# Zero fills of two stages as contiguous megabytes, read from DRAM instead of from SBUF

## The chip, the cores and the metric

The kernel runs on one core of one Trainium2 chip. The metric is device time in microseconds (us) for one execution; lower is better. Three executions of the kernel before took 596.52 to 596.76 us, with a median of 596.55 us. The core has five compute engines (TensorE, called PE in the profile; VectorE, DVE; ScalarE, ACT; GpSimd, POOL; SyncE, SP), an on-chip memory (SBUF) of 128 partitions, and 16 DMA engines which carry all data between SBUF and DRAM. A DMA instruction is issued from one of the compute engines' instruction streams and is then carried out by the DMA engines on their own.

## The reference

One decode step of a transformer block and its gradients: layer norms with a modulation computed from `c`, sliding-window attention over the key and value caches, a gated FFN, and then the vector-Jacobian product for ten inputs.

```python
W = min(4096, max(256, Sk // 4))                # Sk = 65536, so W = 4096
k = jnp.repeat(k_cache[:, :, Sk - W:, :], rep, axis=1)
v = jnp.repeat(v_cache[:, :, Sk - W:, :], rep, axis=1)
p = _softmax(jnp.einsum('bhqd,bhkd->bhqk', q, k) * Dh ** (-0.5), axis=-1)
o = jnp.einsum('bhqk,bhkd->bhqd', p, v)
...
_out, _vjp = jax.vjp(_f, A_x, A_k_cache, A_v_cache, A_wq, A_wo, B_w_gate, B_w_up, B_w_down, c, w_mod)
return (out, *_vjp(grad_out))
```

Only the last 4096 of the 65536 rows of each cache take part. The gradients of the two caches, `out_2` and `out_3`, each of shape (1, 4, 65536, 128) in bf16, are therefore zero in the first 61440 rows of each of the four groups: eight regions of 15.7 MB, 126 MB of zeros in all. The kernel has to write them, and half of what it moves is this.

## The kernel before

**Zeros in pieces.** `zeros` is an SBUF tile of 128 partitions by 2048 fp8 zeros (2 KB per partition). Each of the eight regions is seen as 128 rows of 61440 bf16 elements (120 KB); `region[:, i * ZW:(i + 1) * ZW]` with `ZW = 4096` cuts it into 15 pieces. So a piece is 1 MB that consists of 128 rows of 8 KB, with a step of 120 KB from row to row. There are 120 pieces, in the list `zleft`. A fill (L169) writes a piece seen as fp32 from the fp8 tile: the DMA converts each fp8 zero to an fp32 zero, so that 256 KB are read from SBUF and 1 MB is written to DRAM. Seven of the pieces are narrow (`NARROW`): rows 8 to 127 only (L165), preceded by a small DMA (L162), and the rows left out are written by `zero_rest` (L358 and after).

**When a fill is issued.** `zero(n, after)` issues the next n fills of `zleft` from POOL, in order. The first of them waits for the instruction `after`, so that fills are paced by the work of other engines. Lists by stage (`Z_Q`, `Z_SM`, `Z_N`, `Z_B`, `Z_FOLD`, `Z_FFN`, `Z_END`) say how many fills go where. The order of all instructions is written out by hand.

**The stages.** (1) Loads of the caches' windows, `A_wq` and `w_mod`, with transposes and the projection of q; 4 fills. (2) Scores and softmax; 4 fills. (3) The N stage (L640, `n_ps`), four groups by 32 steps: VectorE scales the values by the probabilities (L193), TensorE multiplies them with the keys. `Z_N` spreads 31 fills over its 128 steps; a fill waits for a matmul a few steps back (`recent(mm, 6)`). Loads of `A_wo` stand between (`load_wo`, L338). (4) The B stage (L695, `b_ps`): `bch` multiplies with `A_wo`, 64 chunks of 8 matmuls. `Z_B` spreads 42 fills over it, each behind a matmul (`recent(mm, 3)`), and between them stand loads of sections of `w_mod` (`wm_sec`, L341) and, near the end, of the first FFN tiles (`load_ug`, L869; `load_wd`, L855, issued from SP). Four more fills lie between the chunks, in calls of their own (`Z_GA`, `Z_CB`). (5) The FFN over seven blocks: each loads its tiles, computes, and stores gradients into the same places (`store_ug`, L873; `store_wd`, L858). (6) The end: gradients of the caches' windows, of `wq`, `wo` and `w_mod`, most of them stores of 512 KB and 1 MB, the last ones issued from SP.

POOL issues DMAs in program order, and one that has to wait holds up all behind it. In the trace POOL's DMAs also wait for the landing of an earlier one, the eighth before, so that up to eight are in flight.

Of the kernel before, what the change touches and what calls it, by code (L numbers as in the profile page):

```python
# [10 lines left out]
P = 128  # L11
FP32 = mybir.dt.float32
BF16 = mybir.dt.bfloat16
FP8 = mybir.dt.float8e4
# [23 lines left out]
NARROW = (15, 45, 75, 93, 103, 113, 119)  # L38

def spread(total, n):
    return [(i + 1) * total // n - i * total // n for i in range(n)]
# [10 lines left out]
Z_N = spread(31, 128)  # L53
Z_B = [n + (i in (31, 38)) for i, n in enumerate(spread(29, 43))] + [1, 1, 1, 1, 0] + [1, 0, 0, 1, 1, 1, 0, 0] + [1, 0, 1, 0, 1, 0, 0, 0]
# [4 lines left out]
def kernel(  # L59
# [26 lines left out]
    nc = tc.nc  # L86
    SKW = A_k_cache.shape[2] - W
# [22 lines left out]
    ZW = 4096  # L110
# [9 lines left out]
    ones_f = vt([P, P], "ones_f")  # L120
    nc.vector.memset(ones_f, 1.0)

    zregions = []
    for og in (out_2, out_3):
        for g in range(G):
            region = og[0, g, 0:SKW, :].rearrange("r d -> (r d)").rearrange("(p x) -> p x", p=P)
            for i in range(region.shape[1] // ZW):
                zregions.append(region[:, i * ZW:(i + 1) * ZW])

    narrow = zregions[0:len(NARROW)]
    wide = zregions[len(NARROW):]
    zleft = []
    while narrow or wide:
        if narrow and (len(zleft) in NARROW or not wide):
# [11 lines left out]
    def dep(later, earlier):  # L147
        tc.add_manual_dep(later.ins, earlier.ins.name,
                          mybir.DependencyInfo(mybir.DependencyClass.Sync, mybir.DependencyReason.DATA),
                          reason="pace")  # L150

    def zero(n, after=None):
        for _ in range(n):
            if len(zleft) <= keep[0]:
                return
            region, narrow_ = zleft.pop(0)
            first = None
            if narrow_:
                nc.gpsimd.inc_swdge_sem([], [], mode="reset_dge_cursor")  # L160
                n = nlen - ncount.pop()
                first = nc.gpsimd.dma_start(  # L162
                    out=rest[0:NS, 0:nlen * 128].rearrange("p (t x) -> p t x", t=2)[:, :, n * 64:(n + 1) * 64],
                    in_=zeros[0:NS, 0:64].rearrange("p (t x) -> p t x", t=1).broadcast_to([NS, 2, 64]))
                ins = nc.gpsimd.dma_start(  # L165
                    out=region[8:P, :].bitcast(FP32).rearrange("(t p) x -> p t x", t=2),
                    in_=zeros[0:60, :].rearrange("p (t x) -> p t x", t=1).broadcast_to([60, 2, ZW // 2]))
            else:
                ins = nc.gpsimd.dma_start(out=region.bitcast(FP32), in_=zeros[:, :])  # L169
            if after is not None:  # L170
                dep(first or ins, after)
# [20 lines left out]
    def tt(out, a, b, op):  # L192
        return nc.vector.tensor_tensor(out=out, in0=a, in1=b, op=op)  # L193
# [215 lines left out]
    for j in range(KD):  # L409
        for k in range(16):  # L410
            mm = nc.tensor.matmul(mod_ps[:, k:k + 1], lhsT=wm01_t[j][:, k * P:(k + 1) * P],
                                  rhs=cs_bf[:, j:j + 1], start=(j == 0 and k == 0), stop=(j == KD - 1),
                                  skip_group_check=True)
# [30 lines left out]
    def bank_pair(name, odd):  # L444
        pair = ((ppq, "pq"), (prq, "rq")) if odd % 2 else ((pna, "na"), (pna, "na"))
        return [pl.tile([P, 512], FP32, name=name, tag=tag) for pl, tag in pair]
# [20 lines left out]
    for j in range(KD):  # L467
# [6 lines left out]
        for h in range(HQ):  # L474
            mm = nc.tensor.matmul(q_ps[:, h:h + 1], lhsT=wq_t[j][:, h * P:(h + 1) * P],
                                  rhs=h1_bf[:, j:j + 1], start=(j == 0 and h == 0), stop=(j == KD - 1),
                                  skip_group_check=True)
# [9 lines left out]
    for ch in range(8):  # L487
        ps = new_ps("sc_ps")
        for g in range(G):
            mm = nc.tensor.matmul(ps[32 * g:32 * g + 32, 0:512], lhsT=q_col2[:, HG * g:HG * g + 32],  # L490
                                  rhs=k_T[:, g, ch * 512:(ch + 1) * 512], start=True, stop=True,
                                  tile_position=(0, 32 * g))
# [75 lines left out]
    def ok_cols(ps):  # L568
        cp(ok_f, ps[:, :])
        okv = ok_ps.rearrange("p (a h) -> p a h", a=2)  # L570
        for g in range(G):
            nc.tensor.matmul(okv[:, :, HG * g:HG * g + HG], lhsT=ok_f[:, g * P:(g + 1) * P],
                             rhs=pair_sel[:, :, HG * g:HG * g + HG], start=True, stop=True)

    def ok_rows():
        cp(o_col, ok_ps[:, 0:HQ])
        cp(kb_col, ok_ps[:, HQ:2 * HQ])
        cp(o_bf, o_col)
        lo = scr[:, 768:832].bitcast(FP32)
        for k, (col, rows, s) in enumerate(((o_col, o_rows, 1.0), (kb_col, nkb_rows, -1.0))):  # L580
            st = st_cols[k].rearrange("p (a h) -> p a h", a=4)
            cp(st[:, 0, :], col)
            tt(lo, col, st[:, 0, :], ALU.subtract)
            cp(st[:, 3, :], lo)
            cp(st[:, 1, :], st[:, 3 - 3 * k, :])
            cp(st[:, 2, :], st[:, 3 * k, :])
            rp = new_tp("rp_ok")[:, 0:P]
            nc.tensor.transpose(rp, st_cols[k], ident_bf[:, :])
            nc.scalar.activation(out=rows, in_=rp, func=ACT.Copy, scale=s)

    def build_bd(g):
        for i in range(HG):
            nc.scalar.activation(out=bd[:, i, :], in_=o_rows, func=ACT.Copy,
                                 scale=sel[:, HG * g + i:HG * g + i + 1])
# [30 lines left out]
    def recent(mm, lag):  # L625
        last_mm.append(mm)
        return last_mm[-lag] if len(last_mm) >= lag else last_mm[0]

    for g in range(G):
        nbank = bank_pair("n_ps", g)  # L630
        for t_ in range(KT):
            s = g * KT + t_
            vp = vp_t[(s // 2) % 2]
            if t_ % 2 == 0:
                tt(vp.rearrange("p t h d -> p (t h d)"),
                   v_nat[:, g, t_ * DH:(t_ + 2) * DH].rearrange("p (t o d) -> p t o d", t=2, o=1).broadcast_to([P, 2, HG, DH]),
                   pT2[:, g, HG * t_:HG * t_ + 2 * HG, :].rearrange("p n (o k) -> p n o k", o=1).broadcast_to([P, 2 * HG, 64, 2]),
                   ALU.mult)
            for k in range(2):
                mm = nc.tensor.matmul(nbank[k][:, :], lhsT=k_nat[:, g, t_ * DH:(t_ + 1) * DH],  # L640
                                      rhs=vp[:, t_ % 2, 4 * k:4 * k + 4, :].rearrange("p h d -> p (h d)"),
                                      start=(t_ == 0), stop=False)
            zero(Z_N[s], recent(mm, 6))
            if t_ == 20:
                build_bd(g)
            if s == 2:
                ok_cols(ok4)
            elif s == 4:
                ok_rows()
            elif s == 24:  # L650
                mod_gb((6, 7))
                load_wo(0)
            elif t_ % 2 == 1:
                side()
        for k in range(2):
            nc.tensor.matmul(nbank[k][:, :], lhsT=nkb_rows[:, :], rhs=bd[:, 4 * k:4 * k + 4, :].rearrange("p h d -> p (h d)"),
                             start=False, stop=True)
            c0 = (HG * g + 4 * k) * P
            nc.scalar.activation(out=N_sb[:, c0:c0 + 512], in_=nbank[k][:, :], func=ACT.Copy, scale=float(SCALE))
        load_wo(4 + g)  # L660
        if g < 3:
            jobs.extend(t_unit(h, "AA") for h in range(HG * g, HG * g + HG))
# [5 lines left out]
    bq = []  # L668
# [13 lines left out]
    nbq = len(bq)  # L682
    bbank = {}

    def bch(n=1):
        for _ in range(n):
            if not bq:
                return
            p, i, u = bq.pop(0)
            if i == 0:  # L690
                bbank[p] = bank_pair("b_ps", p)
            for a in range(4):
                h = 4 * u + a
                for k in range(2):
                    mm = nc.tensor.matmul(bbank[p][k][:, :], lhsT=a4[:, p, h, :], rhs=wo_t[u][:, a, k * 512:(k + 1) * 512],  # L695
                                          start=(i == 0 and a == 0), stop=(i == 7 and a == 3))
            zero(Z_B[nbq - 1 - len(bq)], recent(mm, 3))
            if i == 7:
                for k in range(2):
                    o = B_t[p][:, k * 512:(k + 1) * 512]  # L700
                    if k == 0 or p == NBP - 1:
                        nc.scalar.copy(out=o, in_=bbank[p][k][:, :])
                    else:
                        cp(o, bbank[p][k][:, :])
# [649 lines left out]
```

## Time and profile before

| | |
|---|---|
| median of 3 runs | 596.55 us (596.52 to 596.76) |
| span of the profiled execution, first to last instruction | 594.7 us |
| time outside that span, median less span | 1.85 us |
| bytes moved by DMA | 246.61 MB, mean 415 GB/s |
| read from DRAM / written to it | 60.30 MB / 185.60 MB |
| fills of 1 MB (L169) / of 960 KB (L165) | 113 / 7 |
| busy share PE, DVE, ACT, POOL | 68%, 60%, 44%, 27% |

The profile is of one execution. Its page gives busy shares of each engine over the span, a strip of 40 slices of the span for each engine and for the DMA engines, the queues of the DMA engines (q0 is the one POOL issues to, q1 that of SP and ACT), and the chain of work that ended last. A view of DMA traffic can be taken for any stretch of time; its line "DMA packets" counts the packets that ran in it (one packet is one contiguous piece that one DMA engine moves, and small ones of 4 bytes report completion), the MB, and the mean rate. In a line of the timeline or of a group, the text in square brackets or behind the bar is the idle time before the instruction and what ended it; "x3" is a count. "To landing" is the time from the issue of a DMA to the moment that its completion was reported.

### The profile page before, as it was taken

To read this page: it belongs to the slowest core of one execution; us is meant where nothing else is said; L and a number is where in the kernel's file an instruction comes from. 1 tells how busy PE (TensorE), PEld (TensorE's weight loads), DVE (VectorE), ACT (ScalarE), POOL (GpSimd) and SP (SyncE) were. 2 spreads that over 40 slices of the span, in tenths; PEclk is the share of its full clock that TensorE was granted. 3 is DMA by queue.
4 is the path that set the end of the run, shared out by engine and by line. 5 is a ranking of instruction groups with operands and counts; after the bars stand their busy time and mean duration, and the time that the engine had idled before them with its cause. 6 is when DMAs were issued, how large, how long until landed. Compare 5 with 4: busy or idle time off the path is not lost.

```text
span 594.7 us, 10884 instructions
## 1 busy us (share of the span) xinstructions
PE 403.4 (68%) x4492; PEld 270.3 (45%) x4516; DVE 356.9 (60%) x674; ACT 263.3 (44%) x401; POOL 158.8 (27%) x255
## 2 busy tenths in 40 slices
PE   3997688999999989998866236344455283794510
PEld 3995334334344546544446225334344263593410
DVE  3754499999511010086628686686877884868650
ACT  3489514557211014213125375563665832893310
POOL 3113123222222122223221334223344252223200
PEclk9999699999999999999985566555555576855555
DMA  8999999999999999999999999999999999999997
GB/s 350 420 417 422 412 426 415 429 423 426 426 421 426 422 428 425 423 420 426 418 411 414 418 411 416 409 412 408 399 389 417 420 420 424 421 424 423 425 422 330
DMA packets 44049, 246.61 MB, mean 415 GB/s; under 512 B 5141, under 2 KB 5141, under 8 KB 22552
## 3 DMA queue, kind: packets, MB, share of 16 engines
q0 software_dynamic: 36704, 218.64, 95.5%
q1 hardware_dynamic: 7248, 27.27, 13.0%
q8 instruction: 35, 0.57, 0.4%
q14 instruction: 14, 0.11, 0.0%
q10 hardware_dynamic: 48, 0.01, 0.0%
HBM read 60.30 MB, written 185.60 MB: 413 GB/s over the span
## 4 chain that ended last, share of the span: by engine, by line
PE 36%; DMA 30%; DVE 17%; issue 7%; ACT 5%; POOL 0%; ACTq 0%; DVEq 0%; POOLq 0%; SPq 0%
PE b_ps L695 12%; DMA out_dram<-arena 11%; DMA out_dram<-zeros 6%; PE n_ps L640 6%; DMA arena<-in_B_w_gate_dram 6%; DVE arena L210 5%; DVE arena L206 4%; DVE arena L193 4%; DMA arena<-in_B_w_down_dram 3%; DMA arena<-in_w_mod_dram 3%; PE t_ps L602 2%; PE tp_wq L457 2%; PE w_ps L398 1%; PE tp_side L840 1%; PE tp_k L438 1%
## 5 line engine op out<-in xcount | busy, mean ns | idle before, releaser
L695 PE MATMUL b_ps<-arena 128*128 128x512 bf16 x495 | 113.8, 379 | 2.1 <-ACT arena L841 1.1
L169 POOL DMA_DIRECT2D out_dram<-zeros x113 | 61.7, 547 | 174.5 <-DMA out_dram<-zeros 47.7
L841 ACT COPY arena<-tp_side 128x1024 bf16<-128x1024 bf16 x62 | 60.9, 1014 | 71.7 <-PE tp_side L840 71.7
L193 DVE TENSOR_TENSOR arena<-arena 128x2048 bf16<-128x2048 bf16 x64 | 76.6, 1223 | 2.3 <-PE n_ps L640 0.3
L695 PEld LDWEIGHTS <-arena 128*128 128x128 bf16 x512 | 48.7, 98 | 57.6 <-issue 2.9
L210 DVE CUSTOM_DVE_ANT_0 arena<-arena,scr 128x1024 bf16<-128x1024 bf16 x56 | 66.2, 1221 | 9.9 <-ACT scr L1003 9.9
L640 PE MATMUL n_ps<-arena 128*128 128x512 bf16 x249 | 65.0, 378 | 6.9 <-DVE arena L193 5.0
L840 PE MATMUL tp_side<-ident_bf,arena 128*128 128x128 bf16 x496 | 55.2, 289 | 10.3 <-ACT arena L841 5.1
L840 PEld LDWEIGHTS <-arena 128*128 128x128 bf16 x496 | 47.0, 135 | 16.0 <-issue 9.2
L964 PE MATMUL fg<-h_bf,arena 128*128 128x1 bf16 x448 | 15.6, 166 | 43.3 <-DMA arena<-in_B_w_up_dram 25.2
L640 PEld LDWEIGHTS <-arena 128*128 128x128 bf16 x256 | 24.6, 97 | 41.6 <-issue 16.2
L210 DVE CUSTOM_DVE_ANT_0 arena<-arena,b1k 128x1024 bf16<-128x1024 bf16 x24 | 28.4, 1221 | 20.0 <-PE fg L982 19.9
L873 POOL DMA_DIRECT2D out_dram<-arena x28 | 22.1, 796 | 66.5 <-ACT arena L241 47.7
L241 ACT ACTIVATE arena<-scr,h 128x1024 bf16<-128x1024 bf16 x35 | 38.5, 1143 | 2.7 <-DVE dh2acc L210 2.3
L1183 ACT ACTIVATE arena<-ps_kv 128x512 bf16<-128x512 f32 x48 | 26.2, 686 | 22.5 <-PE ps_kv L1179 22.2
L604 ACT CAST arena<-t_ps 128x512 bf16<-128x512 f32 x56 | 30.1, 589 | 12.1 <-PE t_ps L602 12.1
L964 PEld LDWEIGHTS <-arena 128*128 128x128 bf16 x448 | 14.0, 105 | 45.9 <-DMA arena<-in_B_w_up_dram 26.8
L202 DVE CAST arena<-b_ps 128x512 bf16<-128x512 f32 x6 | 4.1, 692 | 51.1 <-PE b_ps L695 51.1
L1179 PE MATMUL ps_kv<-junk,arena 8*128 8x128 bf16 x256 | 27.6, 306 | 7.9 <-DVE arena L206 7.3
L1179 PEld LDWEIGHTS <-arena 8*128 8x128 bf16 x256 | 25.5, 142 | 10.0 <-issue 9.9
L459 ACT COPY arena<-tp_wq 128x1024 bf16<-128x1024 bf16 x23 | 21.7, 1044 | 8.2 <-PE tp_wq L457 8.2
L982 PE MATMUL fg<-hh_bf,arena 128*128 128x1 bf16 x224 | 8.0, 167 | 21.4 <-DMA arena<-in_B_w_down_dram 20.3
(309 smaller groups left out, 637.9 us busy)
## 6 DMA issues: line engine op xcount, KB each, us to landing
out_dram<-zeros POOLq DMA_DIRECT2D x113, 1024.0 KB, 16.4
out_dram<-arena POOLq DMA_DIRECT2D x28, 1024.0 KB, 17.2
out_dram<-arena POOLq DMA_DIRECT2D x30, 512.0 KB, 10.8
out_dram<-arena SPq DMA_DIRECT2D x20, 512.0 KB, 10.0
arena<-in_A_wq_dram POOLq DMA_DIRECT2D x8, 1024.0 KB, 20.4
arena<-in_A_wo_dram POOLq DMA_DIRECT2D x8, 1024.0 KB, 12.9
arena<-in_w_mod_dram POOLq DMA_DIRECT2D x7, 1024.0 KB, 18.6
arena<-in_B_w_up_dram POOLq DMA_DIRECT2D x14, 512.0 KB, 11.4
```

The costliest lines, as they stand in the source:

```text
L169: ins = nc.gpsimd.dma_start(out=region.bitcast(FP32), in_=zeros[:, :])
L193: return nc.vector.tensor_tensor(out=out, in0=a, in1=b, op=op)
L210: return nc.vector.tensor_tensor_reduce(out=out, in0=w, in1=b, scale=1.0, scalar=0.0, op0=ALU.mult, op1=ALU.add, accum_out=acc)
L241: return nc.scalar.activation(out=out, in_=b, func=ACT.Copy, scale=col)
L604: nc.scalar.copy(out=o, in_=ps)
L640: mm = nc.tensor.matmul(nbank[k][:, :], lhsT=k_nat[:, g, t_ * DH:(t_ + 1) * DH], rhs=vp[:, t_ % 2, 4 * k:4 * k + 4, :].rearrange("p h d -> ...
L695: mm = nc.tensor.matmul(bbank[p][k][:, :], lhsT=a4[:, p, h, :], rhs=wo_t[u][:, a, k * 512:(k + 1) * 512], start=(i == 0 and a == 0), stop= ...
L840: nc.tensor.transpose(tp[:, i * P:(i + 1) * P], blk[:, i * P:(i + 1) * P], ident_bf[:, :])
L841: nc.scalar.copy(out=blk if dst is None else dst, in_=tp[:, :])
L964: nc.tensor.matmul(gu[:, col:col + 1], lhsT=ug_v[:, q % 2, j // 4, j % 4, k, f0:f0 + 255:2], rhs=h2_bf[:, j:j + 1], start=(j == 0 and i == ...
L1179: nc.tensor.matmul(ps[:, t4 * DH:(t4 + 1) * DH], lhsT=rows[32 * g:32 * g + HG, t_ * P:(t_ + 1) * P], rhs=hd[32 * g:32 * g + HG, :], start= ...
L1183: nc.scalar.activation(out=o, in_=ps[:, :], func=ACT.Copy, scale=float(scale))
```

## The change

All pieces but those of the first region (`out_2`, group 0) are now contiguous: the region of 15.7 MB is cut into 15 runs of 1 MB (`flat`). The first region keeps its 15 strided pieces, seven of them narrow.

The first contiguous piece, `zero_src`, is the first fill to be issued, as 128 rows of 8 KB from the SBUF tile. `zero` has a new argument, `big`, set in the two calls in the N stage and in `bch`. A contiguous piece that is filled there is not read from the SBUF tile but from the first 256 KB of `zero_src` in DRAM, seen as fp8, and is written as fp32 as before. On both sides the run is contiguous, so that the DMA is made of sixteen pieces that read 16 KB and write 64 KB each, in place of 128 that read 2 KB and write 8 KB. All other contiguous pieces are written as 128 rows of 8 KB from the SBUF tile. The number of fills, where they are issued, what they wait for and the bytes that they write stay as they were.

```diff
-    zregions = []
+    def fill_rows(og, g):
+        return og[0, g, 0:SKW, :].rearrange("r d -> (r d)")
+
+    first_rows = fill_rows(out_2, 0).rearrange("(p x) -> p x", p=P)
+    NZR = first_rows.shape[1] // ZW
+    zregions = [first_rows[:, i * ZW:(i + 1) * ZW] for i in range(NZR)]
+    flat = []
     for og in (out_2, out_3):
         for g in range(G):
-            region = og[0, g, 0:SKW, :].rearrange("r d -> (r d)").rearrange("(p x) -> p x", p=P)
-            for i in range(region.shape[1] // ZW):
-                zregions.append(region[:, i * ZW:(i + 1) * ZW])
+            if og is not out_2 or g:
+                whole = fill_rows(og, g).rearrange("(i x) -> i x", i=NZR)
+                flat.extend(whole[i:i + 1, :] for i in range(NZR))
+
+    zero_src = flat.pop(0)
+    BIGP = 32
+
+    def as_rows(piece, n):
+        return piece.rearrange("i (p x) -> (i p) x", p=n)
+
+    wide = [as_rows(zero_src, P)] + zregions[len(NARROW):] + flat
     narrow = zregions[0:len(NARROW)]
-    wide = zregions[len(NARROW):]
...
-    def zero(n, after=None):
+    def zero(n, after=None, big=False):
...
+            elif big and region.shape[0] == 1:
+                ins = nc.gpsimd.dma_start(
+                    out=as_rows(region, BIGP).bitcast(FP32),
+                    in_=zero_src[:, 0:P * ZW // 4].rearrange("i (p x) -> (i p) x", p=BIGP).bitcast(FP8))
             else:
+                if region.shape[0] == 1:
+                    region = as_rows(region, P)
                 ins = nc.gpsimd.dma_start(out=region.bitcast(FP32), in_=zeros[:, :])
...
-            zero(Z_N[s], recent(mm, 6))
+            zero(Z_N[s], recent(mm, 6), True)
...
-            zero(Z_B[nbq - 1 - len(bq)], recent(mm, 3))
+            zero(Z_B[nbq - 1 - len(bq)], recent(mm, 3), True)
```

## The prediction

> **What bounds the kernel now.** I read the page's strips first, then the waits of the issuing engine, the chain, and last the DMA traffic of single stretches. The strips (40 slices of 14.9 us; the digit is the busy share in tenths) and the totals:
>
> ```profile
> span 594.7 us, 10884 instructions
> PE   3997688999999989998866236344455283794510
> DMA  8999999999999999999999999999999999999997
> GB/s 350 420 417 422 412 426 415 429 423 426 426 421 426 422 428 425 423 420 426 418 411 414 418 411 416 409 412 408 399 389 417 420 420 424 421 424 423 425 422 330
> DMA packets 44049, 246.61 MB, mean 415 GB/s; under 512 B 5141, under 2 KB 5141, under 8 KB 22552
> HBM read 60.30 MB, written 185.60 MB: 413 GB/s over the span
> ```
>
> The reader should see that the DMA engines are busy from end to end at an almost constant rate, while PE is full in only half of the slices. The time is bytes over rate: 246.61 MB at 415 GB/s are the span. Then who holds up the issuing of fills, from 60 to 320 us (us in total, times, longest), and when fills land (first 80 to 120 us, then 160 to 200 us):
>
> ```profile
> POOL out_dram L169 <- DMA out_dram<-zeros: 39.6, 23, 3.9
> POOL out_dram L169 <- PE n_ps L640: 39.3, 18, 5.7
> POOL out_dram L169 <- PE b_ps L695: 24.5, 10, 5.4
> ...
> DMA to landing us min/median/max: 8.8/13.6/15.8
> ...
> DMA to landing us min/median/max: 15.6/17.4/19.5
> ```
>
> Early on PE paces the fills, but a fill still finds at least 8.8 us of work ahead of it, and this backlog grows to 19.5 us, eight DMAs at some 2.45 us each. Then a fill waits for the eighth DMA before it. So the DMA rate, not the issue, sets the progress. The chain shows where this reaches the compute engines:
>
> ```profile
> 251.16 20.51 DMA out_dram<-zeros
> ...
> 271.95 16.91 DMA out_dram<-zeros
> ...
> 289.41 18.56 DMA arena<-in_w_mod_dram
> ...
> 308.02 1.45 PE g_ps L347 x48
> ...
> 542.65 19.39 DMA out_dram<-arena
> ```
>
> Fills that land late hold the `w_mod` load at 289.41 back, and the FFN begins when it has landed. The end is DMA too:
>
> ```profile
> 290.00:300.00 10.00, 7.23 (x55) 3.94 (x54) 9.48 (x14) 3.04 (x3) 2.56 (x5) 1.00 1.15 410
> ...
> 570.00:580.00 10.00, 0.00 (x0) 0.00 (x0) 2.65 (x4) 0.00 (x0) 0.00 (x0) 0.50 1.02 424
> 580.00:590.00 10.00, 0.00 (x0) 0.00 (x0) 0.00 (x0) 0.00 (x0) 0.00 (x0) 0.50 1.01 420
> ```
>
> (From 290 to 300 us, and 570 to 590 us. Columns: stretch, its length, busy time of PE, weight loads, DVE, ACT, POOL, then clock, DMA share, GB/s.) In the last 20 us nothing but DMA runs.
>
> **The change part by part.** *How many fills.* `Z_N` holds 31, `Z_B` 42. In the order of the list one of the 73 is a strided piece of the first region (number 8) and three are narrow (15, 45, 75). 69 fills become large: 69 MB of the 246.6.
>
> *Packets.* This is the term that counts. The traffic of stretches:
>
> ```profile
> DMA packets 1070, 7.70 MB, mean 428 GB/s; under 512 B 119, under 2 KB 119, under 8 KB 142
> ...
> DMA packets 353, 2.60 MB, mean 433 GB/s; under 512 B 36, under 2 KB 36, under 8 KB 36
> ...
> DMA packets 687, 5.01 MB, mean 417 GB/s; under 512 B 78, under 2 KB 78, under 8 KB 78
> ...
> DMA packets 2828, 18.76 MB, mean 426 GB/s; under 512 B 283, under 2 KB 283, under 8 KB 795
> ```
>
> They are 104 to 122 us and 106 to 112 us (fills, almost alone), 24 to 36 us (loads in 8-KB packets), 106 to 150 us (fills and 512 packets of 4 KB). A fill today takes 1,048,576 B / 428 GB/s = 2.450 us. No row shows a 64-KB packet, so its gain is bounded. If a packet costs a fixed time beside its bytes, a large fill saves seven of them on every DMA engine (one packet instead of eight). In 104 to 122 us, 16 engines x 18,000 ns over 928 packets of 8 KB and 23 of half that make 306.5 ns for 8 KB. In 106 to 150 us that price for 2033 packets leaves 704,000 - 623,100 = 80,900 ns for 512 packets: 158 ns for 4 KB. An 8-KB load takes 192,000 / 609 = 315 ns. Twice 158 less 315 is a fixed cost of 1 ns; at 433 GB/s (303 ns for 8 KB) for the fills the same working gives 172 and 29 ns. Seven packets: 7 to 203 ns per fill, 0.5 to 14 us in all; the upper end would be a fill in 2.25 us, 467 GB/s, which no stretch approaches. The row nearest to a fill without interruptions is the best stretch of fills alone, 433 GB/s: 2.422 us, 28 ns less than now. I take that: 69 x 0.028 = **1.9 us** saved.
>
> The Trainium skill bears on this. "DMA: Bandwidth & Descriptors", section "Why small descriptors are slow (HBM only)", states about three cycles of fixed cost per packet, and its section "Where 436 GB/s comes from" a ceiling of 435 GB/s from 16 ports at 850 MHz. By the first, an estimate: 7 x 3 cycles are 25 ns a fill and 1.7 us in all; by the ceiling a fill takes 2.410 us at best and the gain ends at 2.8 us. The trace's 433 GB/s agrees with the ceiling; that 64-KB packets reach it, no row shows.
>
> *Source in DRAM.* 69 x 256 KB = 18.1 MB more are read from DRAM and as much less from SBUF. Price between nothing and, if read bytes counted like written ones, a quarter of a fill, 0.61 us x 69 = 42 us. Stores that read as much as they write (580 to 590 us) run at 420 GB/s, fills that read a quarter at 428: three quarters of the reading cost 2%, and in 24 to 36 us DRAM itself was the source at 417. Reading runs beside writing; I take nothing and keep both ends.
>
> *Dependence.* A large fill needs `zero_src` written. That is the first fill:
>
> ```profile
> 48.88 0.54 POOL L169 DMA_DIRECT2D out_dram<-zeros  x1 [13.45 <-PE q_ps L475]
> ...
> 74.39 0.53 POOL L169 DMA_DIRECT2D out_dram<-zeros  x1 [5.70 <-PE n_ps L640]
> ```
>
> 25 us lie between it and the first fill of the N stage, more than the 19.5 us of the slowest landing above; the wait costs nothing. If its landing were later, the fills and `load_wo` queued behind on POOL would slip, with 8.8 us of backlog to cover it.
>
> *Issue on POOL.* A fill takes 0.53 us of POOL. With fewer packets it should not rise; if it rose to the 0.77 us of a load (the row of 277.15 below), 69 x 0.24 = 17 us of POOL's time would lie under the same backlog. Nothing. *Other contiguous pieces* (35 outside the two calls) keep 8-KB packets with a step of 8 KB instead of 120 KB. Rows with neither step differ from fills by 2% in both directions at most (420 to 433 GB/s); I take nothing. *The calls' order* and the queues' order are unchanged.
>
> *Other queues.* A packet of SP's queue that alternates with POOL's now may stand behind 64 KB, 2.42 us, not 0.31 us. It matters at the handover to the FFN:
>
> ```profile
> 277.15 0.77 POOL L869 DMA_DIRECT2D arena<-in_B_w_up_dram  x1 [1.99 <-DMA out_dram<-zeros]
> 277.90 0.53 POOL L169 DMA_DIRECT2D out_dram<-zeros  x1
> 279.57 0.77 POOL L869 DMA_DIRECT2D arena<-in_B_w_gate_dram  x1 [1.13 <-DMA out_dram<-zeros]
> 281.95 0.53 POOL L169 DMA_DIRECT2D out_dram<-zeros  x1 [1.62 <-PE b_ps L695]
> ...
> 293.30 0.56 POOL L169 DMA_DIRECT2D out_dram<-zeros  x1 [1.16 <-DMA arena<-in_B_w_up_dram]
> ...
> L341 SPq DMA_DIRECT2D arena<-in_w_mod_dram x2: 328/328/328, 287.0 to 293.4; - x2
> ...
> arena<-in_w_mod_dram SPq DMA_DIRECT2D x4, 256.0 KB, 7.8
> ...
> 308.02 1.44 PE L347 MATMUL g_ps<-cs_bf,arena 128*128 128x1 bf16 x48 [2.86 <-DMA arena<-in_w_mod_dram]
> ...
> q8 instruction: 35, 0.57, 0.4%
> PEld L640 <- issue: 16.2, 35, 1.2
> ```
>
> The last SP load is issued at 293.4, lands at about 301.2 and is needed at 308.02. It has 8 packets per DMA engine (256 KB in 2-KB rows). That it lands in 7.8 us where POOL's load at 289.41 needs 18.56 shows that it passes POOL's backlog. At most four of the eight DMAs in flight at 293.4 are fills, so it comes at most 4 x 2.11 = 8.4 us later, at 309.6. It stays hidden or costs 1.6 us; I take nothing. Code is fetched in 35 packets over the span (the row of q8: packets, MB, share); the trace names no wait for one, and PE's unexplained waits in the N stage are 1.2 us at the longest. A fetch 2.4 us late costs nothing under the backlog.
>
> *Sum.* 594.7 - 1.9 = 592.8 us of span. The runs' median stands 1.85 us above the span; 596.55 - 1.9 = **594.6 us**. What is late next: at 308.02 PE had idled 2.86 us, so the FFN can start at most that much earlier before PE is what it waits for. 1.9 us passes; a saving over 2.9 us would in part only shorten the queue, to be gained later in stages that are DMA-bound.
>
> **The rivals.** (1) *No price per packet.* The low end, 1 ns: fills stay at 2.45 us, the change is worth 0 to 0.5 us, 596.3. For it speaks that 8-KB packets already run at 428 to 433; against, that mixtures with 4 KB run slower (426).
>
> (2) *DRAM becomes slower, and the kernel with it.* In fills alone DRAM is written at 428 GB/s and not read; now it would be read at another 107, and sixteen streams stand 64 KB apart in step. The rate of the slowest of the rows above with fills in it, 410 GB/s, makes a fill 2.557 us: 69 x 0.107 = 7.4 us more, 604.0. It decides from 17 ns per fill on (1.2 us, 0.2%). Against it: no row shows that mixing reading with writing costs more than these few per cent. The Trainium skill's "HBM Reference", section "Specifications (TRN2)", speaks for it with an effective 358 GB/s per core and against it with 716 GB/s per domain, which 428 + 107 leaves free; the trace's 428 is already over the first.
>
> (3) *Reading counts in full*: 596.55 + 42.3 = 638.8. Against: the 2% above.
>
> (4) *Late packets of other queues.* If all eight packets of SP's load met a 64-KB one, it would land 8 x 2.11 = 16.9 us later, at 318.1, 10.1 us after it is needed: 606.6. Against: the mixture in flight. The Trainium skill's "DMA: Bandwidth & Descriptors", section "Queues, rings and completion order", has the engines take turns between queues packet by packet; the 7.8 us agree, the price of turns with 64 KB no run here shows.
>
> **How the numbers follow.** A time within 0.2% (1.2 us) can hardly be told from no change on this kernel. Forecast 0.60; (1) 0.13; (2) 0.12; (3) 0.07; (4) 0.08. Faster 0.60, same 0.13, slower 0.27. The forecast's own range is 592 to 595.3: its low end is 4.5 us saved, a fill in 2.385 us. The whole range goes from 591.5 to 601.0 and leaves out (3), half of (2) and (4) and a little below: about 0.2.
>
> **What the profile after would show.** Right: 69 x 112 = 7728 fewer packets on q0; DRAM reading up from 60.3 to about 78.4 MB; 430 GB/s or more in the N and B stages; less waiting of POOL for the eighth DMA before; the `w_mod` load behind the last fills issued about 2 us before 289.41; an end at 420 GB/s as now. Wrong: fills that land later than 19.5 us with a rate below 425 in N and B (2, 3); PE waiting longer than 2.86 us ahead of `g_ps`, for an SP load (4); the same rate as now (1). A wait on each large fill for another large fill's data would overturn everything; the diff has no such overlap.

## The result, and the profile after

The kernel after takes 595.53 us (median of 20 runs, 595.15 to 597.43) against 596.54 us before (20 runs): 1.0 us less, a ratio of 0.9984 with a 95% interval of 0.9978 to 0.9990. It is faster, by a sixth of a per cent, which lies inside the 0.2% that the prediction called hard to tell from no change; only the many runs make it visible. The forecast was 1.9 us less, 594.6 us; 595.53 lies 0.2 us above its own range (592 to 595.3) and inside the whole range (591.5 to 601.0). The profiled execution has a span of 593.8 us, 0.9 us below that of before.

The strips and totals of the page after:

```profile
span 593.8 us, 10908 instructions
PE   3997789999999989998876236344455294894410
DMA  9999999999999999999999999999999999999997
GB/s 351 421 416 422 412 461 393 448 429 427 426 421 403 442 446 411 443 425 402 412 418 402 418 413 414 411 409 405 398 392 418 420 417 426 418 423 426 425 421 328
DMA packets 36321, 246.61 MB, mean 415 GB/s; under 512 B 5141, under 2 KB 5141, under 8 KB 22552
q0 software_dynamic: 28976, 218.64, 91.8%
HBM read 78.39 MB, written 185.60 MB: 445 GB/s over the span
```

The queue of POOL before:

```profile
q0 software_dynamic: 36704, 218.64, 95.5%
```

The bytes that count (246.61 MB) and the small packets are the same. q0 carries 28,976 packets where it carried 36,704: 7728 fewer, 69 x 112. DRAM is read for 18.1 MB more. The strip of GB/s jumps between 393 and 461 in the N and B stages because a packet of 64 KB is counted whole in the slice where it starts; the mean is what can be read. The line "DMA packets" of a stretch counts in the same way: whole packets, those that start in it.

The two long stages, 76 to 300 us: DMA traffic before, then after:

```profile
DMA packets 15209, 94.80 MB, mean 423 GB/s; under 512 B 1661, under 2 KB 1661, under 8 KB 5527
```

```profile
DMA packets 7931, 95.29 MB, mean 425 GB/s; under 512 B 1673, under 2 KB 1673, under 8 KB 5638
```

After has moved 0.49 MB more in the same 224 us. At 425 GB/s this is 1.15 us, some 18 ns for each of the 65 large fills that start in it. Counting a packet that is under way by the share of it that is done, the lead at 300 us is 0.41 MB, 1.0 us, 14 ns for each of the 69. It grows evenly from 0.02 MB at 80 us to 0.24 MB at 180 us and 0.41 MB at 300 us, and it is 0.43 MB at 500 us: the gain is made fill by fill in these stages and then neither lost nor increased.

The chain at the handover to the FFN, and PE's wait there (idle before in brackets), after:

```profile
247.63 19.20 DMA out_dram<-out_dram
267.12 18.36 DMA out_dram<-zeros
...
289.60 17.37 DMA arena<-in_w_mod_dram
307.01 1.45 PE g_ps L364 x48
...
307.01 1.44 PE L364 MATMUL g_ps<-cs_bf,arena 128*128 128x1 bf16 x48 [2.14 <-DMA arena<-in_w_mod_dram]
```

`g_ps` starts at 307.01 instead of 308.02 us: the 1.0 us has arrived. PE still waits 2.14 us for the load, so the limit that the prediction set at 2.86 us was not reached. The `w_mod` load itself is issued no earlier (289.60 against 289.41 us); it lands sooner (17.37 against 18.56 us).

### The profile page after: what moved, and what is told of

Read it like the earlier page. It is cut to its first block, busy times and chain, and to the rows that moved or that the text cites. A ratio compares the mean times of both kernels' runs of the same rounds, so it can differ in the third digit from the quotient of the medians.

```text
span 593.8 us, 10908 instructions
## 1 busy us (share of the span) xinstructions
PE 406.3 (68%) x4516; PEld 271.3 (46%) x4516; DVE 356.7 (60%) x674; ACT 263.6 (44%) x401; POOL 156.2 (26%) x255
## 2 busy tenths in 40 slices
DMA packets 36321, 246.61 MB, mean 415 GB/s; under 512 B 5141, under 2 KB 5141, under 8 KB 22552
## 3 DMA queue, kind: packets, MB, share of 16 engines
q0 software_dynamic: 28976, 218.64, 91.8%
## 4 chain that ended last, share of the span: by engine, by line
DMA 47%; PE 19%; DVE 17%; issue 6%; ACT 5%; POOL 1%; ACTq 0%; DVEq 0%; POOLq 0%; SPq 0%
DMA out_dram<-arena 16%; DMA out_dram<-out_dram 16%; PE n_ps L657 6%; DMA arena<-in_B_w_gate_dram 6%; DVE arena L227 5%; DVE arena L223 5%; DVE arena L210 4%; DMA arena<-in_B_w_down_dram 3%; DMA out_dram<-zeros 3%; DMA arena<-in_w_mod_dram 3%; ACT arena L476 2%; PE t_ps L619 2%; PE w_ps L415 1%; PE tp_k L455 1%; PE b_ps L712 1%
## 5 line engine op out<-in xcount | busy, mean ns | idle before, releaser
L712 PE MATMUL b_ps<-arena 128*128 128x512 bf16 x512 | 115.9, 379 | 1.1 <-ACT arena L858 1.1
L180 POOL DMA_DIRECT2D out_dram<-out_dram x69 | 34.1, 495 | 118.6 <-PE n_ps L657 36.0
L186 POOL DMA_DIRECT2D out_dram<-zeros x44 | 24.8, 565 | 56.8 <-PE q_ps L492 16.1
## 6 DMA issues: line engine op xcount, KB each, us to landing
arena<-in_A_wo_dram POOLq DMA_DIRECT2D x8, 1024.0 KB, 13.2
```

The source lines that it names most:

```text
L180: ins = nc.gpsimd.dma_start(out=as_rows(region, BIGP).bitcast(FP32), in_=zero_src[:, 0:P * ZW // 4].rearrange("i (p x) -> (i p) x", p=BIGP ...
```

## Experiments

**One part at a time.** The change does three things to a large fill: its place is contiguous, its source is DRAM, and its packets are larger. The prediction held packets to be the cause; the rivals here are the other two. The first kernel has the layout alone.

```diff
-            zero(Z_N[s], recent(mm, 6), True)
+            zero(Z_N[s], recent(mm, 6))
...
-            zero(Z_B[nbq - 1 - len(bq)], recent(mm, 3), True)
+            zero(Z_B[nbq - 1 - len(bq)], recent(mm, 3))
```

> The changed layout alone: all pieces outside the first region contiguous, but every fill still made of 128 rows of 8 KB from the SBUF tile. If the gain of the change (596.54 to 595.53 us) comes from larger packets, this one is at 596.5 us and its packets on q0 number 36,704 as before. If it comes from the contiguous layout (a step of 8 KB instead of 120 KB), it is at 595.5 us. If it comes from the DRAM source: 596.5 us.

The other kernels of this series write the four regions of `out_3` in `NROW` rows per piece, strided over the region as before, and read DRAM. 60 fills are of this kind; the other 9 come from the SBUF tile. With `NROW = 128` a row has 8 KB, as before the change.

```diff
+                if og is out_3:
+                    cut = fill_rows(og, g).rearrange("(p x) -> p x", p=NROW)
+                    strided.extend(cut[:, i * ZROW:(i + 1) * ZROW] for i in range(NZR))
...
-                    out=as_rows(region, BIGP).bitcast(FP32),
-                    in_=zero_src[:, 0:P * ZW // 4].rearrange("i (p x) -> (i p) x", p=BIGP).bitcast(FP8))
+                    out=region.bitcast(FP32),
+                    in_=zero_src[:, 0:P * ZW // 4].rearrange("i (p x) -> (i p) x", p=NROW).bitcast(FP8))
```

> 60 of the 69 large fills as 128 rows of 8 KB with a step of 120 KB (the shape of before), but read from DRAM; the other 9 as before. It isolates the source at the old packet size. Larger packets as the cause: 596.5 us, a fill at 2.450 us as before. The DRAM source as the cause: 60 x 14.5 ns = 0.9 us less, 595.7 us (14.5 ns a fill is the lead of 0.42 MB that the changed kernel has by 300 us, over 69 fills at 425 GB/s). If reading from DRAM costs and the larger packets only make up for it: slower than 596.5 us, by 60 times what a packet loses, 8 packets a fill per DMA engine; 10 ns a packet would be 4.8 us, 601.3 us.

> The same 60 fills as 64 rows of 16 KB from DRAM. By a fixed cost per packet and a neutral source: 4 of the 7 saved packets, 60 x 8.3 ns = 0.5 us less than before, 596.0 us. By the source alone: 595.7 us. By the layout alone: 596.5 us. If the DRAM source costs a fixed time per packet: half of the loss of the kernel with 8 KB.

> The same 60 fills as 32 rows of 32 KB from DRAM. By a fixed cost per packet and a neutral source: 6 of the 7 saved packets, 60 x 12.4 ns = 0.7 us less than before, 595.8 us. By the source alone: 595.7 us. By the layout alone: 596.5 us. If the DRAM source costs a fixed time per packet: a quarter of the loss of the kernel with 8 KB.

Then the other direction, rows smaller than before:

> The 60 fills in 256 rows of 4 KB from DRAM: 8 more packets per fill on each DMA engine. At the 2.1 ns per packet that the changed kernel gained (14.5 ns for 7 packets): 60 x 17 ns = 1.0 us more than before, 597.6 us. At 14 ns per packet, the middle of what the mixture of packets in the trace of before allowed: 60 x 112 ns = 6.7 us more, 603.3 us. Without a price per packet: 596.6 us.

> The 60 fills in 512 rows of 2 KB from DRAM: 24 more packets per fill on each DMA engine than before. At 2.1 ns per packet: 60 x 50 ns = 3.0 us more than before, 599.6 us. At 14 ns: 60 x 336 ns = 20 us more, 616.8 us. Without a price per packet: 596.6 us.

Measured, in order of packet size (ratio to the kernel before from runs on the same chip):

| kernel | packets of the fills | median us | before | ratio, 95% interval | lead at 300 us, MB |
|---|---|---|---|---|---|
| 60 fills, 2 KB from DRAM | 512 a fill | 601.28 | 596.54 | 1.0080 (1.0066 to 1.0094) | -1.92 |
| 60 fills, 4 KB from DRAM | 256 | 598.04 | 596.54 | 1.0026 (1.0015 to 1.0037) | -0.60 |
| layout alone, 8 KB from SBUF | 128 | 596.65 | 596.60 | 1.0003 (0.9994 to 1.0012) | -0.05 |
| 60 fills, 8 KB from DRAM | 128 | 596.55 | 596.60 | 0.9998 (0.9990 to 1.0007) | -0.03 |
| 60 fills, 16 KB from DRAM | 64 | 596.01 | 596.60 | 0.9995 (0.9986 to 1.0004) | +0.18 |
| 60 fills, 32 KB from DRAM | 32 | 596.09 | 596.60 | 0.9990 (0.9981 to 0.9998) | +0.31 |
| the change, 69 fills, 64 KB from DRAM | 16 | 595.53 | 596.54 | 0.9984 (0.9978 to 0.9990) | +0.41 |

The last column is the lead over the kernel before in bytes moved, from one profile each, with a packet under way counted by the share that is done. The ratios are on record as worked out from all runs; they need not be those of the medians (16 KB: 0.9990 by the medians).

Layout and source change nothing: both stand within 0.1 us and 0.05 MB of before. That the cause is the number of packets follows from the row of sizes: in the five kernels that read DRAM with 60 fills, only the rows' number and length change, and with them the step from row to row, which the kernel with the layout alone shows to cost nothing at 8 KB. The times show a price below 8 KB and for 64 KB; at 16 and 32 KB they hardly leave the noise, but the leads keep the order of the sizes there too.

POOL's time for an issue falls along the row, too, from 622 ns (2 KB) over 556, 525 and 504 to 498 (32 KB) and 495 ns (64 KB), but it is not the cause: with 8 KB from DRAM it is 22 ns shorter than the 547 ns of before, 1.3 us over 60 fills, and nothing is gained; with 4 KB it is 9 ns longer, 0.5 us, and 1.5 us are lost.

Divided by the packets added or saved on each DMA engine: 2 KB, 4.74 us / (60 x 24) = 3.3 ns a packet; 4 KB, 1.50 / (60 x 8) = 3.1 ns; 64 KB, 1.01 / (69 x 7) = 2.1 ns. (16 and 32 KB by their medians give 2.5 and 1.4 ns, with intervals about as wide as the effect.) The traffic from 76 to 300 us with rows of 2 KB and of 4 KB shows the same loss:

```profile
DMA packets 37701, 92.90 MB, mean 415 GB/s; under 512 B 1602, under 2 KB 1602, under 8 KB 35774
```

```profile
DMA packets 22690, 94.20 MB, mean 421 GB/s; under 512 B 1644, under 2 KB 1644, under 8 KB 20696
```

2.5 times the packets of before in the same stretch cost 2% of its rate: a packet is cheap here. The DMA packet records show why a price is hard to read from single durations. These are the shortest and the commonest durations of the fills' packets, from 76 to 300 us:

```
packet   shortest   commonest
 8 KB      322 ns     348 ns
16 KB      624        649
32 KB     1226       1226, 1252
64 KB     2431       2431
```

Each shortest duration is a constant of about 21 ns beside 602.6 ns per 16 KB, which over 16 engines are 435 GB/s. The commonest ones up to 32 KB are 25 to 26 ns longer, but consecutive packets overlap: eight of 348 ns would be 2.78 us, and a fill takes 2.45. So neither 21 nor 47 ns is what a packet costs; overlap leaves 2 to 3 ns of it.

**What reading costs.** Rivals (2) and (3) of the prediction priced reading from DRAM at up to 42 us. At 256 KB a fill it costs nothing (the row of 8 KB above). Two kernels read more: 512 KB of bf16 zeros, or the whole MB.

```diff
-                    in_=zero_src[:, 0:P * ZW // 4].rearrange("i (p x) -> (i p) x", p=BIGP).bitcast(FP8))
+                    in_=as_rows(zero_src[:, 0:P * ZW // 2], BIGP))
```

```diff
-                    out=as_rows(region, BIGP).bitcast(FP32),
-                    in_=zero_src[:, 0:P * ZW // 4].rearrange("i (p x) -> (i p) x", p=BIGP).bitcast(FP8))
+                    out=as_rows(region, BIGP),
+                    in_=as_rows(zero_src, BIGP))
```

> The 69 large fills read a whole MB of zeros from DRAM (64 KB read and 64 KB written by a packet, no conversion) instead of 256 KB. If reading runs beside writing and DRAM has room: as the changed kernel, 595.5 us, a fill at 2.44 us. If read bytes count like written ones: a fill moves 2 MB at 428 GB/s, 4.9 us, 69 x 2.45 = 169 us more, 765 us. By the Trainium skill's HBM Reference, section Specifications (TRN2), 716 GB/s per domain are a ceiling below the 860 GB/s that free reading would need: 2 MB in 2.93 us, 69 x 0.48 = 33 us more, 630 us; an estimate from that page.

> The 69 large fills read 512 KB of bf16 zeros from DRAM and write 1 MB of fp32 zeros: between the changed kernel (256 KB, 595.5 us) and the one that reads 1 MB (629.7 us). If DRAM traffic has a ceiling: a fill of 1.5 MB at 2.44 us is 645 GB/s, and the kernel that reads 1 MB reached 721 GB/s in its median packet (64 KB read and 64 KB written in 2909 ns on each of 16 DMA engines); the ceiling isn't reached, 595.5 us. If each MB that is read has a price: (629.7 - 595.5) x 0.25 / 0.75 = 11.4 us more, 606.9 us.

The kernel that reads 512 KB takes 595.33 us (ratio 0.9984, 0.9975 to 0.9993), the same as the change. The one that reads 1 MB takes 629.72 us (ratio 1.0553, 1.0537 to 1.0569). DMA traffic from 76 to 300 us, first with 512 KB, then with 1 MB:

```profile
DMA packets 7907, 95.14 MB, mean 425 GB/s; under 512 B 1668, under 2 KB 1668, under 8 KB 5619
```

```profile
DMA packets 6156, 82.78 MB, mean 370 GB/s; under 512 B 1388, under 2 KB 1388, under 8 KB 4204
...
HBM read 132.65 MB, written 185.60 MB: 507 GB/s over the span
```

So up to 512 KB read bytes do not count; only the last step is slower. Its packets spread from 2418 to 4240 ns with a median of 2875 ns (2909 ns from 76 to 300 us): the fastest run at the full rate, the median one at 64 KB read and 64 KB written in 2909 ns, 721 GB/s over 16 engines. With 512 KB a fill asks for 1.5 MB in 2.44 us, 645 GB/s, and gets it. This fits a ceiling on what DRAM reads and writes together, but not a sharp one: in the eight stretches of 10 us between 80 and 300 us in which these fills ran almost alone (at most 0.06 MB of other traffic), reading and writing made 639 to 748 GB/s, 696 on average. Where loads made up most of the traffic, the packets ran at the full rate (a median of 2418 ns from 210 to 220 us). So a large packet that reads 64 KB is not slow by itself, nor because it converts nothing, the other thing that this edit changes; it was slow where most of the traffic was packets like it. Whether DRAM's total is the limit or, for example, the common step of 64 KB at which sixteen of them read and write, was not tried. The Trainium skill's "HBM Reference", section "Specifications (TRN2)", gives 716 GB/s per domain. The median packet's 721 GB/s lie near it and the stretches on both sides of it; the 630 us estimated from it before the run came out at 629.7, though the rate was not constant. That two cores share this bandwidth, as the Trainium skill says, no run here shows.

**What the large packets hold up.** Rival (4) was that packets of other queues wait behind 64 KB. It is there in the kernel after: the `w_down` loads issued from SP between 283 and 312 us, before and after (count, size, median us to landing):

```profile
arena<-in_B_w_down_dram SPq DMA_DIRECT2D x2, 512.0 KB, 8.8
```

```profile
arena<-in_B_w_down_dram SPq DMA_DIRECT2D x2, 512.0 KB, 13.2
```

Each view has the landing of one of the two loads. By the completion records of the trace, the first took 12.7 us before and 13.2 after, the second 8.8 and 13.2. So the second lands 4.4 us later, and nobody is seen to wait for it. In the FFN such loads would be needed. One kernel makes all 104 contiguous fills large, another does this too but with 16-KB packets for the last 30, which are those of the FFN and the end.

```diff
-    def zero(n, after=None, big=False):
+    def zero(n, after=None, big=True):
```

> All 104 contiguous fills read from DRAM in sixteen packets of 64 KB, those of the FFN and of the end too. If a fill's 14.5 ns are all that the packet size does: 104 x 14.5 ns = 1.5 us less than before, 595.0 us, half a us faster than the changed kernel. If packets of other queues are held up behind 64 KB: the w_down loads issued from SP, which already land after 13.2 instead of 8.8 us at the handover in the changed kernel, are late in each of the six blocks that follow; one to two fills per block in flight, 2 us each, make 2 to 4 us per block, 12 to 24 us in all: 608 to 620 us.

> All contiguous fills read from DRAM as in the kernel that has them all large (596.6 us), but the last 30 of the list, which are those of the FFN and of the end, are made of 64 packets of 16 KB instead of 16 of 64 KB. If the 1.1 us that the kernel with all fills large lost to the changed one come from packets of SP's queue that wait behind 64 KB: a wait is a quarter as long, the loss all but goes, and 4 packets fewer than before per DMA engine and fill save 30 x 8.3 ns = 0.2 us: 595.3 us. If they come from the DRAM source or the layout in these stages: 596.6 us.

With all fills large: 596.62 us (ratio 0.9999, 0.9991 to 1.0008), so the gain is gone. With 16 KB there: 595.71 us (ratio 0.9985, 0.9976 to 0.9994), as good as the change and no better. From 310 to 480 us the landings of SP's stores and PE's waits for `w_down` and `w_up` (us, times, longest) are, in the kernel after, in the one with all fills large, and in the one with 16 KB:

```profile
out_dram<-arena SPq DMA_DIRECT2D x14, 512.0 KB, 9.8
...
PE fg L981 <- DMA arena<-in_B_w_up_dram: 26.2, 10, 6.6
...
PE fg L999 <- DMA arena<-in_B_w_down_dram: 19.6, 7, 5.8
```

```profile
out_dram<-arena SPq DMA_DIRECT2D x14, 512.0 KB, 13.7
...
PE fg L999 <- DMA arena<-in_B_w_down_dram: 27.4, 9, 9.0
...
PE fg L981 <- DMA arena<-in_B_w_up_dram: 14.4, 7, 5.8
```

```profile
out_dram<-arena SPq DMA_DIRECT2D x14, 512.0 KB, 10.7
...
PE fg L1010 <- DMA arena<-in_B_w_down_dram: 25.5, 8, 6.2
...
PE fg L992 <- DMA arena<-in_B_w_up_dram: 18.3, 8, 4.0
```

With all fills large a store lands 3.9 us later, and PE waits 7.8 us more for `w_down`. But this wait is not the price: PE waits 11.8 us less for `w_up`, and with 16-KB packets the wait for `w_down` is nearly as long (25.5 us) while the time is good. The time follows the bytes. At 560 us the kernel after and the one with 16 KB both lead the kernel before by 0.43 MB, and the one with all fills large is 0.14 MB behind it; these 0.57 MB are 1.4 us at some 415 GB/s. It falls back from 340 to 380 us, where the DMA engines move 390 and 379 GB/s (in two stretches of 20 us) against 415 and 412 in the kernel after, and makes up a part later. So the 12 to 24 us that were expected did not come: what counts is the work that the DMA engines lack, not how long PE waits. The cure by shorter packets, with the source still in DRAM, shows that the source is not what did it, and the kernel after, whose FFN fills are contiguous too, that the layout is not; the packets' length remains. Which late store or load left the DMA engines short was not taken apart.

## Why the prediction was right, and where its size was off

*DMA rate sets the progress.* Right. Fills that take 0.6% less time in one part of the span move the end by the same 1.0 us, with no compute engine's own work touched.

*Packets, 69 x 28 ns = 1.9 us.* Right in kind, and shown by the row of sizes; the measured size was half of it. The mis-sized term is the 28 ns: a fill gained 14 to 18 ns. The saving of 1.0 us lies between the forecast and rival (1), no price per packet (596.3 us, at most 0.5 us saved), and nearer to the rival; it is the row of sizes, and not the time alone, that decides for a price. The row that the 28 ns came from was the best short stretch, 433 GB/s, 2.60 MB in 6 us. A stretch that short holds two and a half fills, and whole packets that fall in or out at its ends move its rate by some per cent. With the packets at its ends counted by the share that lies inside, this stretch ran at 427.8 GB/s, and no stretch of 6 us between 76 and 300 us at more than 427.9. The extra rate was therefore one of counting, and that a gain read from it came within a factor of two is luck. Counted by shares, the 18 us of fills from 104 to 122 us went from 427.1 to 429.5 GB/s, 2.455 to 2.441 us a fill: 14 ns. How little whole packets tell in 6 us, the same stretch of the kernel after shows, with 410 GB/s where the shares give 430.0:

```profile
DMA packets 78, 2.46 MB, mean 410 GB/s; under 512 B 37, under 2 KB 37, under 8 KB 37
```

Over 224 us the rates were 423 and 425. The fit that was made beside it (1 to 29 ns a packet from mixtures of packets) had the true 2 to 3 ns near its lower end. By the Trainium skill's "DMA: Bandwidth & Descriptors", section "Why small descriptors are slow (HBM only)", three cycles a packet, the prediction's estimate was 1.7 us. Three cycles at the 850 MHz of the Trainium skill's ceiling are, as an estimate, 3.5 ns: the 3.1 and 3.3 ns of the small packets agree with it, and the 2.1 ns of the large ones (1.2 to 2.7 by the interval) fall short of it.

*Source in DRAM, nothing.* Right at 256 KB a fill, and up to 512 KB. The argument for it (stores that read as much as they write run only 2% slower) was not enough by itself: it concerns reading from SBUF, and with a whole MB from DRAM the time rose by 33 us. Rival (2) expected a loss already at 256 KB a fill; the loss came only at 1 MB, and that DRAM's total makes it fits but is not shown.

*Dependence, issue on POOL, other contiguous pieces: nothing.* The first two were not tried by themselves; the sum leaves no room for them, and an issue now takes less of POOL. The group of fills before, and that of the large fills after:

```profile
L169 POOL DMA_DIRECT2D out_dram<-zeros x113 | 61.7, 547 | 174.5 <-DMA out_dram<-zeros 47.7
...
L180 POOL DMA_DIRECT2D out_dram<-out_dram x69 | 34.1, 495 | 118.6 <-PE n_ps L657 36.0
```

0.50 instead of 0.55 us on average. The layout alone made 596.65 against 596.60 us.

*Other queues, hidden or 1.6 us.* Hidden. By the completion records, the last `w_mod` load from SP took 9.5 us (293.14 to 302.67) instead of 8.3 (293.42 to 301.71), well within the 8.4 us more that were allowed, and PE needs it at 307.01. Rival (4) is real, as the second `w_down` load shows, but it costs time only in the FFN, where this change makes no large fills.

*What the profile would show.* Packets and DRAM bytes came out as said. Wrong were the 430 GB/s (425), the earlier issue of the `w_mod` load (it moved its landing), and the lesser waiting of POOL for earlier DMAs. From 60 to 320 us after:

```profile
POOL out_dram L180 <- DMA out_dram<-out_dram: 30.5, 18, 3.5
...
POOL out_dram L180 <- DMA out_dram<-zeros: 5.4, 3, 2.2
POOL out_dram L186 <- DMA out_dram<-out_dram: 6.0, 4, 1.8
```

These are 41.9 us, where the row of before had 39.6. The waits are how POOL spends the time between its paced issues; they do not measure the DMA rate.

## What to carry to other kernels

Where the DMA engines are busy from end to end, what a packet costs is worth knowing, but from 8 KB up it is hardly worth removing: going from 8 to 64 KB for 69 MB gave 1.0 us, while going down to 2 KB for 60 MB cost 4.7 us. Size such a term from a stretch of hundreds of microseconds, or count the packets at a stretch's ends by their share; do not take the best few microseconds. Large packets make the packets of other queues wait, so keep them out of stages in which a short load or store on another queue is on the path.

## What was not expected of the hardware

A DMA that reads DRAM and writes DRAM ran at the full rate while it read 256 or 512 KB per MB written (425 GB/s of traffic in both), and fell to 370 GB/s when it read as much as it wrote, with 639 to 748 GB/s of reading and writing together where such fills ran almost alone. And the source made no difference at equal packet size: 8-KB packets from DRAM took 322 and 348 ns, exactly as from SBUF.
